# Reordering the first layer norm of a DiT block: x tile 3 ahead of tile 2, chunk 0's scale by itself, filler matmuls

## The chip, the cores and the metric

The kernel runs on one core of a Trainium2 chip. Its time is the time on the device for one execution, in microseconds (us); of several executions the median is given. Beside it stands the span, from the first to the last instruction of one profiled execution. Matmuls run on TensorE (PE in the profile; PEld is its weight load), elementwise work on VectorE (DVE), ScalarE (ACT) and GpSimd (POOL), and SyncE (SP) issues nearly all loads.

## The reference

One DiT block on x of 2 x 256 x 1152 (bf16), with a conditioning vector c per batch. Only the beginning matters here:

```python
mod = (_silu(c) @ w_mod).reshape(B, 6, 1, D)
shift_a, scale_a, gate_a, shift_m, scale_m, gate_m = [mod[:, i] for i in range(6)]
h = _layernorm(x, axis=-1) * (1 + scale_a) + shift_a
qkv = (h @ wqkv).reshape(B, N, 3, H, Dh)
...
x = x + gate_a * a
h2 = _layernorm(x, axis=-1) * (1 + scale_m) + shift_m
m = _gelu(h2 @ w_fc1) @ w_fc2
return x + gate_m * m
```

B is 2, N 256, D 1152, there are two heads of 576, and w_fc1 has 4608 columns. Between the lines shown stand softmax attention and the output projection wo.

## The kernel before

The 512 rows of x are four tiles of 128 rows (tiles 0 and 1 are batch 0, tiles 2 and 3 batch 1); the 1152 columns are nine chunks of 128. The kernel goes through the block in order: statistics and norm of x, k, shift, q, scores, softmax, v, attention, wo, second norm, fc1, fc2. It is written as straight-line code, and each engine executes its instructions in the order in which the source issues them (the loop at lines 777 to 787 fixes that by hand). So a wait at the head of an engine's queue holds all that stands behind it there.

What happens in the first 25 us:

- SP issues the four tiles of x (lines 85 and 86), then in turn pieces of w_scale_a (line 107: the columns for chunks 0 and 1, 2 and 3, 4 and 5, 6 and 7, and 8) and of w_k (line 104), all on one queue, with no wait between them.
- TensorE multiplies zeros in fp32 (`warm`, line 171), two times and later eight times more. Their result is not used.
- The statistics of tiles 0 and 2 are made on ScalarE: two passes with a running sum, of the difference to the row's first element and of its square (`act_stats`, line 202). VectorE and Pool make mean and variance of the sums (`act_mean`, `act_var`). Tiles 1 and 3 use bn_stats on VectorE, in three pieces of 384 columns (`stats_piece`).
- The inverse root for tiles 0 and 1 is a power on Pool (line 324), the one for tiles 2 and 3 is Ln and Exp on ScalarE (`ln_exp_rsqrt`).
- `norm1` writes the normalised tile xn on VectorE, the first 512 columns first (four chunks), the rest later. TensorE transposes it chunk by chunk into PSUM (`transpose_x`, line 258).
- `scale_group` makes the scale of some chunks: for each chunk nine matmuls of the weights w_scale_a with the vector silu(c), two columns wide (line 244). One is added on the way to SBUF, on ScalarE for chunks 0 and 1 (line 250), on VectorE for the others (line 251).
- `modulate` multiplies a transposed chunk of one batch (256 columns) by its scale while copying it from PSUM to hT0, on VectorE (line 264) or ScalarE (line 266). hT0 lies in the tile named big in the profile. The shift is left for later.
- `k_step(k, ...)` multiplies chunk k of hT0 with w_k for six accumulators pk of PSUM (line 274), for one batch or for both. PSUM has six accumulator buffers ("acc") and two for transposes and scales ("aux").

Chunks 0 to 3 are done batch by batch, in an order written out by hand at lines 332 to 362; from chunk 4 on a loop alternates scale group, transposes, modulation and k step, up to the evacuation of k.

Of the kernel before, what the change touches and what calls it, by code (L numbers as in the profile page):

```python
# [9 lines left out]
BF16 = mybir.dt.bfloat16  # L10
ACT = mybir.ActivationFunctionType
ALU = mybir.AluOpType
# [3 lines left out]
LN_EPS = 1e-5  # L16
# [3 lines left out]
def kernel(  # L20
# [11 lines left out]
    nc = tc.nc  # L32
    B, N, D = x.shape
# [3 lines left out]
    P = 128  # L37
    T = B * N
    NT = T // P
    TPB = N // P  # L40
    KD = D // P
# [11 lines left out]
    const = ctx.enter_context(tc.tile_pool(name="const", bufs=1))  # L53
# [6 lines left out]
    def acc_tile(shape, name, dt=FP32):  # L60
        return psum.tile(shape, dt, name=name, tag="acc", bufs=6)

    def aux_tile(shape, name, dt=FP32):
        return psum.tile(shape, dt, name=name, tag="aux", bufs=2)
# [17 lines left out]
    x_sb = act.tile([P, NT, D], BF16, name="x_sb", tag="x_sb")  # L82
    c_sb = act.tile([B * KD, P], BF16, name="c_sb")
    nc.scalar.dma_start(c_sb[:], c_v)
    for t in range(NT):
        nc.sync.dma_start(x_sb[:, t, :], x_v[:, t // TPB, t % TPB, :])  # L86

    zeros = const.tile([P, T], BF16, name="zeros")
# [10 lines left out]
    KM1 = 6  # L99
# [45 lines left out]
    hT0 = aT  # L145
# [11 lines left out]
    neg_half = const.tile([P, B], FP32, name="neg_half")  # L157
# [2 lines left out]
    nc.gpsimd.tensor_tensor(early[:], eps_t[:], neg_half[:, 0:1], op=ALU.pow)  # L160
    ones = const.tile([P, 1], FP32, name="ones")
    nc.gpsimd.memset(ones[:], 1.0)
    pc = aux_tile([P, B * KD], "pc", BF16)
    pwarm = acc_tile([P, T], "pwarm")

# [3 lines left out]
    def warm(n, dst):  # L169
        for _ in range(n):  # L170
            nc.tensor.matmul(dst[:, 0:T // 2], zeros32[:, 0:P], zeros32, start=True, stop=True)  # L171
# [13 lines left out]
    mv1 = small.tile([P, NT, 2], FP32, name="mv1", tag="mv1", bufs=1)  # L185
    rstd1 = small.tile([P, NT], FP32, name="rstd1", tag="rstd1", bufs=1)
# [3 lines left out]
    def stats_piece(t, j):  # L190
        nc.vector.bn_stats(stats1[t][:, j, :], x_sb[:, t, j * PW:(j + 1) * PW])
        if j == NPD - 1:
            nc.vector.bn_aggr(mv1[:, t, :], stats1[t][:].rearrange("p a b -> p (a b)"))


    dsum = small.tile([P, NT], FP32, name="dsum", tag="dsum", bufs=1)
    dsq = small.tile([P, NT], FP32, name="dsq", tag="dsq", bufs=1)
    dm2 = small.tile([P, NT], FP32, name="dm2", tag="dm2", bufs=1)

    def act_stats(t):  # L200
        for f, dst in ((ACT.Identity, dsum), (ACT.Square, dsq)):
            nc.scalar.activation(
                xns[t][:], x_sb[:, t, :], f, bias=x_sb[:, t, 0:1], scale=-1.0,
                accum_out=dst[:, t:t + 1],
            )

    def act_mean(t, eps):
        one = slice(t, t + 1)
        nc.vector.scalar_tensor_tensor(
            dm2[:, one], dsum[:, one], -1.0 / (D * D), dsum[:, one], op0=ALU.mult, op1=ALU.mult  # L210
        )
        if eps:
            nc.gpsimd.tensor_scalar_add(dm2[:, one], dm2[:, one], LN_EPS)
        nc.gpsimd.tensor_scalar(
            mv1[:, t, 0:1], dsum[:, one], -1.0 / D, x_sb[:, t, 0:1], op0=ALU.mult, op1=ALU.add
        )

    def act_var(t):
        one = slice(t, t + 1)
        nc.vector.scalar_tensor_tensor(  # L220
            mv1[:, t, 1:2], dsq[:, one], 1.0 / D, dm2[:, one], op0=ALU.mult, op1=ALU.add
        )

    def pair(t):
        return mv1[:, t:t + 2, 1:2].rearrange("p t o -> p (t o)"), rstd1[:, t:t + 2]

    def ln_exp_rsqrt(dst, var):
        nc.scalar.activation(dst, var, ACT.Ln, bias=eps_t[:], scale=1.0)
        nc.scalar.activation(dst, dst, ACT.Exp, scale=-0.5)

    def norm1(t, c0, c1):
        nc.vector.tensor_scalar(
            xns[t][:, c0:c1], x_sb[:, t, c0:c1], mv1[:, t, 0:1], rstd1[:, t:t + 1],
            op0=ALU.subtract, op1=ALU.mult,
        )


    scale_a = act.tile([P, KD, B], FP32, name="scale_a")

    def scale_group(k0, k1, tile_of=aux_tile):  # L240
        pm = tile_of([P, k1 - k0, B], "pm")
        for j in range(k0, k1):
            for k in range(KD):
                nc.tensor.matmul(  # L244
                    pm[:, j - k0, :], w_scale_a[:, k, j * P:(j + 1) * P], sT[:, k, 0:B],
                    start=(k == 0), stop=(k == KD - 1),
                )
        dst = scale_a[:, k0:k1, :]
        return lambda: (
            nc.scalar.activation(dst, pm[:], ACT.Identity, bias=ones[:]) if k0 == 0  # L250
            else nc.vector.tensor_scalar_add(dst, pm[:], 1.0)
        )

    def transpose_x(ks, ts):
        pt = aux_tile([P, len(ks), len(ts) * P], "pt", BF16)
        for j, t in enumerate(ts):
            for i, k in enumerate(ks):
                nc.tensor.transpose(pt[:, i, j * P:(j + 1) * P], xns[t][:, k * P:(k + 1) * P], ident[:])
        return pt

    def modulate(pt, i, k, b, j0, eng):
        dst, src, sc = hT0[:, k, b * N:(b + 1) * N], pt[:, i, j0:j0 + N], scale_a[:, k, b:b + 1]
        if eng == "d":
            nc.vector.tensor_scalar_mul(dst, src, sc)  # L264
        else:
            nc.scalar.mul(dst, src, sc)
# [3 lines left out]
    def k_step(k, c0=0, c1=T, m0=0, m1=KM1):  # L270
        for m in range(m0, m1):
            if k == 0 and c0 == 0:
                pk[m] = acc_tile([P, T], "pk")
            nc.tensor.matmul(  # L274
                pk[m][:, c0:c1], w_k[:, k, m * P:(m + 1) * P], hT0[:, k, c0:c1],
                start=(k == 0 and c0 == 0), stop=(k == KD - 1), skip_group_check=True,
            )
# [30 lines left out]
    CUT = 4 * P  # L308
    BT = [range(b * TPB, (b + 1) * TPB) for b in range(B)]

    def both(pt, k):
        for b, e in enumerate("da"):
            modulate(pt, 0, k, b, b * N, e)

    warm(8, pwarm)
    act_stats(0)
    act_stats(2)
    for j in range(NPD):
        stats_piece(1, j)
    act_mean(0, True)  # L320
    nc.gpsimd.tensor_scalar_add(mv1[:, 1, 1:2], mv1[:, 1, 1:2], LN_EPS)
    act_var(0)
    var, rstd = pair(0)
    nc.gpsimd.tensor_tensor(rstd, var, neg_half[:], op=ALU.pow)
    stats_piece(3, 0)
    norm1(0, 0, CUT)
    norm1(1, 0, CUT)
    stats_piece(3, 1)
    act_mean(2, False)
    stats_piece(3, 2)  # L330
    act_var(2)
    pt_a = transpose_x([0, 1], BT[0])
    add = scale_group(0, 2)
    add()
    modulate(pt_a, 0, 0, 0, 0, "d")
    var, rstd = pair(2)
    ln_exp_rsqrt(rstd, var)
    modulate(pt_a, 1, 1, 0, 0, "a")
    norm1(2, 0, CUT)
    norm1(3, 0, CUT)  # L340
    k_step(0, 0, N)
    k_step(1, 0, N, 0, 3)
    pt_c = transpose_x([0, 1], BT[1])
    modulate(pt_c, 0, 0, 1, 0, "d")
    modulate(pt_c, 1, 1, 1, 0, "a")
    norm1(0, CUT, D)
    norm1(1, CUT, D)
    k_step(1, 0, N, 3, KM1)
    k_step(0, N, T)
    add = scale_group(2, 4)  # L350
    pt_b = transpose_x([2, 3], BT[0])
    add()
    modulate(pt_b, 0, 2, 0, 0, "d")
    modulate(pt_b, 1, 3, 0, 0, "a")
    norm1(2, CUT, D)
# [6 lines left out]
    k_step(2, N, T)  # L362
    for k in range(3, KD):
        if k in (3, 5, 7):
            scale_group(k + 1, min(k + 3, KD))()
        if k < KD - 1:
            both(transpose_x([k + 1], range(NT)), k + 1)
        k_step(k)
# [143 lines left out]
    def attn_transpose(i):  # L512
        pair = attn_all[:, TPB * i:TPB * (i + 1), :].rearrange("p i n -> p (i n)")
        return nc.scalar.dma_start_transpose(attnT_all[:, i, :].rearrange("p (c n) -> p c n", n=P), pair)
# [242 lines left out]
    for gi, (n, t, c0, cw) in enumerate(groups):  # L757
# [3 lines left out]
        for kk in range(KF):  # L761
            j, r = divmod(n * KF + kk, 27)
# [3 lines left out]
                start=(kk == 0), stop=(kk == KF - 1),  # L766
# [11 lines left out]
    for ins in list(nc.cur_bb.bb.instructions)[first_traced:]:  # L778
        eng = ins.engine
# [38 lines left out]
```

## Time and profile before

| What | Value |
|---|---|
| Median of 4 runs | 244.13 us (243.87 to 245.23) |
| Profiled execution | 244.45 us |
| Its span | 242.7 us |
| Granted TensorE clock, mean | 1.000 |
| Bytes through the DMA queues | 53.29 MB, 220 GB/s on average |
| Landings of x tiles 0, 1, 2, 3 | 3.54, 4.28, 6.16, 7.10 us |
| Landings of w_scale_a, chunks 0-1 and 6-7 | 9.25 and 20.01 us |

All times of day in this document count from the span's start. The page of the profile gives first the busy time of each engine, then the same in 40 slices of the span, the DMA queues, the chain of work that ended last, and the costliest groups of instructions. The lines of an order of time are: start, length, engine, source line, operation, output<-input, shapes and number of instructions; in brackets the engine's idle time before it and what ended it. A busy TensorE is not TensorE at its peak. A matmul's length holds its latency too; where matmuls follow each other, what counts is the step from start to start.

### The profile page before, as it was taken

The page shows a single profiled execution, that of the slowest core. Times are in us where ns is not written, and L with a number is a line of the kernel's source. Part 1 is how long each engine was busy: PE and PEld are TensorE (multiplying, and loading weights), DVE is VectorE, ACT ScalarE, POOL GpSimd, SP SyncE. Part 2 cuts the span into 40 slices and gives each one's busy share as a digit, 9 for nine tenths or more (in the row PEclk, how much of TensorE's full clock was granted, in tenths as well). Part 3 has the DMA queues.
Part 4 walks back from the last instruction along what each step waited for, and adds up shares of the span by engine and source line. Part 5 has one row for each costly group of instructions (what it writes and reads, how often), then busy time and mean ns, then how long its engine had stood idle before and what let it go on. Part 6 is the DMA issues. An engine that isn't in the chain of part 4 may idle for free.

```text
span 242.7 us, 3988 instructions
## 1 busy us (share of the span) xinstructions
PE 237.0 (98%) x1698; PEld 145.5 (60%) x1698; DVE 91.1 (38%) x192; ACT 59.8 (25%) x120; POOL 27.8 (11%) x45
## 2 busy tenths in 40 slices
PE   8899999999999999999999999999999999999994
PEld 5775444466567666888854444444665665665674
DVE  4652442318416578831002999960010000000001
ACT  6632332307214032672422223332000000000000
POOL 2200000001400333200000000001121111111111
PEclk9999999999999999999999999999999999999999
DMA  6999999996499999239999999999200000000000
GB/s 204 316 319 319 379 365 392 389 393 215 99 307 397 389 375 153 41 65 340 392 389 393 343 327 297 261 327 296 97 16 16 20 16 16 19 18 16 26 25 16
DMA packets 48781, 53.29 MB, mean 220 GB/s; under 512 B 9587, under 2 KB 36475, under 8 KB 48763
## 3 DMA queue, kind: packets, MB, share of 16 engines
q1 hardware_dynamic: 41312, 50.14, 62.3%
q10 hardware_dynamic: 6939, 1.71, 5.1%
q0 software_dynamic: 512, 1.19, 1.8%
q8 instruction: 13, 0.21, 0.4%
q14 instruction: 5, 0.04, 0.1%
HBM read 50.14 MB, written 1.19 MB: 212 GB/s over the span
## 4 chain that ended last, share of the span: by engine, by line
PE 90%; SPq 4%; DMA 4%; issue 0%; DVE 0%; DVEq 0%
PE pacc L763 29%; PE pacc L707 29%; PE pacc L654 7%; PE pacc L563 7%; PE pq L485 7%; DMA w_scale_a<-in_w_mod_dram 4%; SPq L104 3%; PE pk L303 2%; PE pk L274 2%; PE pa L603 2%; PE ps_s L520 2%; PE pn L380 2%; SPq L86 1%; SPq L107 1%; PE pg L462 0%; PE pm L244 0%
## 5 line engine op out<-in xcount | busy, mean ns | idle before, releaser
L707 PE MATMUL pacc<-hT,w_f 128*128 128x256 bf16 (+1 forms) x432 | 70.5, 326 | 0.0
L763 PE MATMUL pacc<-w_f,gT 128*128 128x384 bf16 (+2 forms) x468 | 70.5, 314 | 0.0
L763 PEld LDWEIGHTS <-gT 128*128 128x128 bf16 x468 | 44.4, 98 | 26.2
L707 PEld LDWEIGHTS <-w_f 128*128 128x128 bf16 x432 | 42.2, 98 | 27.6
L769 DVE TENSOR_TENSOR tmp<-pacc,gate 128x384 f32<-128x384 f32 (+2 forms) x13 | 6.9, 527 | 65.6 <-PE pacc L763 57.3
L739 ACT ACTIVATE gT<-pacc 128x512 bf16<-128x512 f32 x24 | 14.3, 597 | 32.6 <-PE pacc L707 32.6
L433 DVE SCALAR_TENSOR_TENSOR part<-w_gate_m,s,part 128x1152 f32<-128x1152 bf16 x16 | 21.4, 1414 | 0.0
L654 PE MATMUL pacc<-w_o,big 128*128 128x384 bf16 x108 | 17.9, 326 | 0.0
L771 POOL TENSOR_TENSOR o_sb<-tmp,x 128x384 bf16<-128x384 f32 (+1 forms) x12 | 11.7, 971 | 54.0 <-DVE tmp L769 54.0
L485 PE MATMUL pq<-hT,w_q 128*128 128x512 bf16 x81 | 17.8, 379 | 0.0
L563 PE MATMUL pacc<-w_v,hT 128*128 128x384 bf16 x108 | 17.7, 326 | 0.0
L563 PEld LDWEIGHTS <-hT 128*128 128x128 bf16 x108 | 10.5, 98 | 7.1 <-issue 0.3
L654 PEld LDWEIGHTS <-big 128*128 128x128 bf16 x108 | 10.4, 98 | 7.2 <-issue 0.4
L274 PE MATMUL pk<-big,w_k 128*128 128x256 bf16 (+1 forms) x72 | 13.3, 326 | 0.9 <-DVE big L264 0.8
L485 PEld LDWEIGHTS <-w_q 128*128 128x128 bf16 x81 | 7.8, 98 | 9.4
L660 POOL TENSOR_TENSOR x<-tmp,x_sb 128x384 f32<-128x384 f32 x8 | 7.3, 913 | 27.1 <-DMA w_scale_m<-in_w_mod_dram 15.2
L431 DVE TENSOR_SCALAR part<-w_gate_m,s 128x1152 f32<-128x1152 bf16 x2 | 1.6, 819 | 21.9 <-DMA w_gate_m<-in_w_mod_dram 21.9
L274 PEld LDWEIGHTS <-w_k 128*128 128x128 bf16 x72 | 6.7, 98 | 4.5 <-issue 1.1
L171 PE MATMUL pwarm<-zeros 128*128 128x256 f32 x20 | 7.8, 564 | 1.2 <-DVE eps_t L93 1.2
L455 POOL DMA_DIRECT2D gates_dram<-nat_v x2 | 1.1, 534 | 67.6 <-DVE nat_v L453 67.6
L728 ACT ACTIVATE gT<-pacc 128x512 bf16<-128x512 f32 x12 | 6.5, 598 | 9.0 <-PE pacc L707 9.0
L476 POOL DMA_DIRECT2D gates_dram<-nat x4 | 2.3, 577 | 52.1 <-DVE nat L473 51.5
(94 smaller groups left out, 163.9 us busy)
## 6 DMA issues: line engine op xcount, KB each, us to landing
w_f<-in_w_fc_dram SPq DMA_DIRECT2D x12, 864.0 KB, 14.4
w_f<-in_w_fc_dram SPq DMA_DIRECT2D x3, 1728.0 KB, 7.9
w_f<-in_w_fc_dram SPq DMA_DIRECT2D x2, 2592.0 KB, 17.3
w_gate_a<-in_w_mod_dram SPq DMA_DIRECT2D x3, 864.0 KB, 11.7
w_v<-in_wqkv_dram SPq DMA_DIRECT2D x3, 864.0 KB, 13.9
w_o<-in_wo_dram SPq DMA_DIRECT2D x3, 864.0 KB, 14.0
w_shift_m<-in_w_mod_dram SPq DMA_DIRECT2D x3, 864.0 KB, 8.6
w_scale_m<-in_w_mod_dram SPq DMA_DIRECT2D x3, 864.0 KB, 13.3
```

Of the source, the lines that this page charges most:

```text
L104: nc.sync.dma_start(w_k[:, k0:k1, c0:c1], wqkv_v[:, k0:k1, D + c0:D + c1])
L171: nc.tensor.matmul(dst[:, 0:T // 2], zeros32[:, 0:P], zeros32, start=True, stop=True)
L274: nc.tensor.matmul(pk[m][:, c0:c1], w_k[:, k, m * P:(m + 1) * P], hT0[:, k, c0:c1], start=(k == 0 and c0 == 0), stop=(k == KD - 1), skip_g ...
L433: nc.vector.scalar_tensor_tensor(part[:, b, :], wg[:, k, :], s32[:, k, b:b + 1], part[:, b, :], op0=ALU.mult, op1=ALU.add,)
L485: nc.tensor.matmul(pq[m][:], w_q[:, k, m * P:(m + 1) * P], hT[:, k, :], start=(k == 0), stop=(k == KD - 1), skip_group_check=True,)
L563: nc.tensor.matmul(pacc[:], hT[:, k, t * P:(t + 1) * P], w_v[:, k, pnl * PW:(pnl + 1) * PW], start=(k == 0), stop=(k == KD - 1),)
L654: nc.tensor.matmul(pacc[:], aT[:, k, t * P:(t + 1) * P], w_o[:, k, c0:c1], start=(k == 0), stop=(k == KD - 1),)
L660: (nc.gpsimd if pool_add else nc.vector).tensor_tensor(x1[:, t, c0:c1], tmp[:], x_sb[:, t, c0:c1], op=ALU.add)
L707: nc.tensor.matmul(dst, w_f1[m // KD][:, k, ml * P:(ml + 1) * P], hT[:, k, c0:c1], start=start, stop=(k == KD - 1), **kw,)
L739: nc.scalar.activation(gT[:, m, :], pacc[:], ACT.Gelu_apprx_tanh)
L763: nc.tensor.matmul(pacc[:], gT[:, kk, t * P:(t + 1) * P], w_f2[j][:, r, c0 - n * PW:c0 - n * PW + cw], start=(kk == 0), stop=(kk == KF - 1),)
L771: (nc.vector if last else nc.gpsimd).tensor_tensor(o_sb[:], tmp[:], x1[:, t, c0:c0 + cw], op=ALU.add)
```

## The change

The change touches only what is issued in the first 13 us or so:

- x tile 3 is loaded ahead of tile 2.
- Tile 3's statistics are all issued ahead of the first norms; its inverse root is a power on Pool, by itself. Tile 2's stays with Ln and Exp on ScalarE, for one column instead of two.
- Tile 1 is normed ahead of tile 0, tile 3 ahead of tile 2.
- The scales of chunks 0 and 1 are two groups, with accumulators of the "acc" kind. Chunk 0's starts with a matmul of a row of ones, so that PSUM holds one plus the scale; VectorE multiplies the chunk of batch 0 by it straight from PSUM, and ScalarE copies it to SBUF later. Chunk 1's one is added on ScalarE as before, and its half of batch 0 is multiplied on VectorE instead of ScalarE.
- Two matmuls of zeros (128x512, bf16) are put into TensorE's order, one behind the scale matmuls and one behind tile 3's transposes.
- The transposes of chunks 0 and 1 for tile 3 stand ahead of the first k step, those for tile 2 between the first and the second; the second k step of batch 0 is no longer cut in two.

The core of the diff:

```diff
-    for t in range(NT):
+    for t in (0, 1, 3, 2):
         nc.sync.dma_start(x_sb[:, t, :], x_v[:, t // TPB, t % TPB, :])
...
+    ones_row = const.tile([1, P], BF16, name="ones_row")
+    nc.gpsimd.memset(ones_row[:], 1.0)
...
         for j in range(k0, k1):
+            if j == 0:
+                nc.tensor.matmul(pm[:, 0, :], ones_row[:], ones_row[:, 0:B], start=True, stop=False)
             for k in range(KD):
                 nc.tensor.matmul(
                     pm[:, j - k0, :], w_scale_a[:, k, j * P:(j + 1) * P], sT[:, k, 0:B],
-                    start=(k == 0), stop=(k == KD - 1),
+                    start=(k == 0 and j > 0), stop=(k == KD - 1),
                 )
...
+    def fill(n):
+        for _ in range(n):
+            nc.tensor.matmul(pwarm[:], zeros[:, 0:P], zeros[:], start=True, stop=True)
+
+    def pool_eps(t):
+        nc.gpsimd.tensor_scalar_add(mv1[:, t, 1:2], mv1[:, t, 1:2], LN_EPS)
+
+    def pool_rsqrt(t0, t1):
+        nc.gpsimd.tensor_tensor(
+            rstd1[:, t0:t1], mv1[:, t0:t1, 1:2].rearrange("p t o -> p (t o)"),
+            neg_half[:, 0:t1 - t0], op=ALU.pow,
+        )
...
-    act_mean(0, True)
-    nc.gpsimd.tensor_scalar_add(mv1[:, 1, 1:2], mv1[:, 1, 1:2], LN_EPS)
+    act_sq_mean(0)
+    nc.gpsimd.tensor_scalar_add(dm2[:, 0:1], dm2[:, 0:1], LN_EPS)
+    pool_eps(1)
+    stats_piece(3, 0)
     act_var(0)
-    var, rstd = pair(0)
-    nc.gpsimd.tensor_tensor(rstd, var, neg_half[:], op=ALU.pow)
-    stats_piece(3, 0)
+    pool_rsqrt(0, 2)
+    act_mean(0)
+    stats_piece(3, 1)
+    stats_piece(3, 2)
+    pool_eps(3)
+    pool_rsqrt(3, 4)
+    norm1(1, 0, CUT)
     norm1(0, 0, CUT)
-    norm1(1, 0, CUT)
-    stats_piece(3, 1)
-    act_mean(2, False)
-    stats_piece(3, 2)
+    pt_a = transpose_x([0, 1], BT[0])
+    act_sq_mean(2)
+    act_mean(2)
+    norm1(3, 0, CUT)
+    pm0, pm1 = [scale_group(k, k + 1, acc_tile) for k in range(2)]
     act_var(2)
-    pt_a = transpose_x([0, 1], BT[0])
-    add = scale_group(0, 2)
-    add()
-    modulate(pt_a, 0, 0, 0, 0, "d")
-    var, rstd = pair(2)
-    ln_exp_rsqrt(rstd, var)
-    modulate(pt_a, 1, 1, 0, 0, "a")
+    nc.vector.tensor_scalar_mul(hT0[:, 0, 0:N], pt_a[:, 0, :], pm0[:, 0, 0:1])
+    scale_add(pm1, 1, 2, "a")
+    modulate(pt_a, 1, 1, 0, 0, "d")
+    ln_exp_rsqrt(rstd1[:, 2:3], mv1[:, 2, 1:2])
+    nc.scalar.copy(scale_a[:, 0:1, :], pm0[:])
     norm1(2, 0, CUT)
-    norm1(3, 0, CUT)
+    fill(1)
+    pt_c = aux_tile([P, 2, N], "pt", BF16)
+    transpose_x([0, 1], [3], pt_c, 1)
+    fill(1)
     k_step(0, 0, N)
-    k_step(1, 0, N, 0, 3)
-    pt_c = transpose_x([0, 1], BT[1])
+    transpose_x([0, 1], [2], pt_c, 0)
+    k_step(1, 0, N)
     modulate(pt_c, 0, 0, 1, 0, "d")
     modulate(pt_c, 1, 1, 1, 0, "a")
     norm1(0, CUT, D)
     norm1(1, CUT, D)
-    k_step(1, 0, N, 3, KM1)
     k_step(0, N, T)
```

`act_mean` is split into `act_sq_mean` (VectorE) and `act_mean` (Pool), and the adding of the one is now `scale_add`; both do what they did.

More of the change, by code (lines that the diff above doesn't have):

```diff
@@ L205, in act_stats, with act_sq_mean @@
             )
-    def act_mean(t, eps):
+    def act_sq_mean(t):
         one = slice(t, t + 1)
@@ L211, in act_mean @@
         )
-        if eps:
-            nc.gpsimd.tensor_scalar_add(dm2[:, one], dm2[:, one], LN_EPS)
+    def act_mean(t):
         nc.gpsimd.tensor_scalar(
-            mv1[:, t, 0:1], dsum[:, one], -1.0 / D, x_sb[:, t, 0:1], op0=ALU.mult, op1=ALU.add
+            mv1[:, t, 0:1], dsum[:, t:t + 1], -1.0 / D, x_sb[:, t, 0:1], op0=ALU.mult, op1=ALU.add
         )
@@ L222, in act_var @@
         )
-    def pair(t):
-        return mv1[:, t:t + 2, 1:2].rearrange("p t o -> p (t o)"), rstd1[:, t:t + 2]
     def ln_exp_rsqrt(dst, var):
@@ L245, in scale_group, with scale_add, transpose_x @@
                     pm[:, j - k0, :], w_scale_a[:, k, j * P:(j + 1) * P], sT[:, k, 0:B],
-                    start=(k == 0), stop=(k == KD - 1),
+                    start=(k == 0 and j > 0), stop=(k == KD - 1),
                 )
[L248 to L256, printed above, removed]
+        return pm
+    def scale_add(pm, k0, k1, eng="d"):
+        if eng == "a":
+            nc.scalar.activation(scale_a[:, k0:k1, :], pm[:], ACT.Identity, bias=ones[:])
+        else:
+            nc.vector.tensor_scalar_add(scale_a[:, k0:k1, :], pm[:], 1.0)
+    def transpose_x(ks, ts, pt=None, j0=0):
+        if pt is None:
+            pt = aux_tile([P, len(ks), len(ts) * P], "pt", BF16)
+        for j, t in enumerate(ts, j0):
             for i, k in enumerate(ks):
@@ L347 @@
     norm1(1, CUT, D)
-    k_step(1, 0, N, 3, KM1)
     k_step(0, N, T)
-    add = scale_group(2, 4)
+    pm = scale_group(2, 4)
     pt_b = transpose_x([2, 3], BT[0])
-    add()
+    scale_add(pm, 2, 4)
     modulate(pt_b, 0, 2, 0, 0, "d")
@@ L364 @@
         if k in (3, 5, 7):
-            scale_group(k + 1, min(k + 3, KD))()
+            k1 = min(k + 3, KD)
+            scale_add(scale_group(k + 1, k1), k + 1, k1)
         if k < KD - 1:
```

## Prediction

> **What bounds the kernel now.** I read the page first, then the chain of waits, then the order of time of TensorE, VectorE and ScalarE over the first 21 us, and last the DMA queue around 18 us. From the page:
>
> ```profile
> span 242.7 us, 3988 instructions
> PE 237.0 (98%) x1698; PEld 145.5 (60%) x1698; DVE 91.1 (38%) x192; ACT 59.8 (25%) x120; POOL 27.8 (11%) x45
> ```
>
> TensorE is idle for only 5.7 us: 1.2 before its first matmul, about 3 after its last one, and 1.3 in between. The matmul idle in between lies wholly before 21 us, in the stretch that the change edits. So no edit of it can win more than that, and what it wins must survive to the first point where TensorE waits for something else. Two lines of TensorE's order of time show the two places (start, length, engine, line, operation; in brackets the idle time before and what ended it):
>
> ```profile
> 9.29 0.60 PE L244 MATMUL pm<-sT,w_scale_a 128*128 128x2 bf16 x18
> 10.70 1.14 PE L274 MATMUL pk<-big,w_k 128*128 128x256 bf16 x9 [0.80 <-DVE big L264]
> ...
> 18.21 1.46 PE L274 MATMUL pk<-big,w_k 128*128 128x512 bf16 x6
> 20.05 0.60 PE L244 MATMUL pm<-sT,w_scale_a 128*128 128x2 bf16 x18 [0.38 <-DMA w_scale_a<-in_w_mod_dram]
> ```
>
> The first idle, 0.80, is what the change works on. The second is a DMA: the scale columns for chunks 6 and 7 land at 20.01. The chain of waits (start, length, what) agrees, and it does not go through 10.70 at all:
>
> ```profile
> 11.20 8.81 DMA w_scale_a<-in_w_mod_dram
> 20.01 0.05 issue
> 20.05 0.60 PE pm L244 x18
> 20.66 0.25 PE pt L258 x4
> 20.90 1.29 PE pk L274 x6
> ```
>
> Behind 20.05 the chain is TensorE's own work down to 239.5 us. The last matmul ahead of 20.05 starts at 19.293 and the next could start 0.216 later (the step between 512-column matmuls there), at 19.51. So TensorE arrives 0.54 early in this execution: **slack 0.54**.
>
> **The change, part by part.** Where a step has the same semaphore latency as now, I keep the offset that the trace shows (0.02 to 0.09).
>
> *x tile 3 ahead of tile 2.* SP issues the same four loads (0.38 to 0.43 each) ahead of the same weights, so the weight queue does not move. The landings are 3.54, 4.28, 6.16 and 7.10; tiles 3 and 2 swap the last two. Tile 3's three bn_stats on VectorE start at 6.18 instead of 7.12, and step by 0.47. Tile 2's two ScalarE passes start at 7.12 instead of 6.20; two passes with their reads took from 6.20 to 8.91, 2.71, so the square sum is there at 9.83.
>
> *Statistics ahead of the norms.* VectorE: bn_stats at 6.18, tile 0's variance at 6.65 (its square sum is there at 6.30), two bn_stats to 7.77, the aggregate to 8.04 (0.24; the next one can follow 0.15 after its start). Pool's root for tiles 0 and 1 (0.72) starts at about 6.9 as now and ends at 7.61, the mean at 7.87 (0.26), and both are hidden by the bn_stats. The norms of tiles 1 and 0 (0.41 each, stepping by 0.33) run from 7.96 to 8.69 instead of 7.68 to 8.41. TensorE's transposes need both: 0.28 later for VectorE. It costs nothing, because the warming matmuls hold TensorE until 8.876 in any case (8.69 plus 0.05 to the weight load plus 0.1 is 8.84). This cover is thin: 0.03.
>
> *Root of tile 3 on Pool.* The addition of eps costs 0.20 and the root lies between 0.58 (the 128x1 root of line 160) and 0.72 (the 128x2 one). From 8.04: ready at 8.95 to 9.1. Tile 3's norm runs to about 9.5 instead of 11.51. Pool has nothing else to do; tile 2's mean behind it takes 0.26, and is wanted only at 10.7.
>
> *Chunk 0's scale alone.* Now the 18 scale matmuls end at 9.90, ScalarE adds one, and only then VectorE multiplies:
>
> ```profile
> 10.00 0.26 ACT L250 ACTIVATE scale_a<-pm,ones 128x4 f32<-128x4 f32 x1 [1.08 <-PE pm L244]
> ...
> 10.30 0.35 DVE L264 TENSOR_SCALAR big<-pt,scale_a 128x256 bf16<-128x256 bf16 x1 [0.60 <-ACT scale_a L250]
> ```
>
> With the one added by a matmul with a row of ones (one more 25 ns step beside 18; its weight load 0.1 lies in the 0.20 wait for the weights), nine matmuls end at 9.7 and VectorE reads the scale from PSUM. But tile 2's variance stands ahead in VectorE's queue and waits for the square sum at 9.83. So it runs at 9.86 and the multiplication at 9.95 to 10.30. Its price with a scalar from PSUM no row shows: between 0.35 (the same shape here) and 0.51 (with the 0.16 of the small PSUM read of line 251 on top); I take 0.35, the same operation and shape. The first k matmul can start at 10.35 instead of 10.70.
>
> *Fillers.* Two matmuls of 512 columns, 0.216 each at the step seen from 16.7 on (0.427 if the clock were at its early half). After the scale matmuls (last start 9.73): filler, two transposes of tile 3 (0.055 each), filler: done at 10.4. They lie in the wait for VectorE and cost 0.05 of it at most, 0.5 in the slow case.
>
> *Order of the k steps.* The first matmuls now run at 10.40 to 11.05. VectorE multiplies chunk 1 (0.35, at 10.3, the scale from ScalarE at 10.26), and norms tile 2 when its root is there: Ln follows ScalarE's scale at 10.16, Exp ends at 10.68, norm 10.73 to 11.15. Transposes at 11.2, chunk 1's six matmuls 11.3 to 12.0. VectorE's first half-tile of batch 1 is done at 11.9, just ahead of TensorE. ScalarE's late copy of chunk 0's scale (0.16 to 0.26, about 10.9) releases the sixth accumulator, wanted at 10.95: 0 to 0.05. The second six end at 12.6, and the next scale group, which started at 13.159, starts at about **12.62: 0.54 earlier**. That takes in the 0.115 idle at 12.5, which goes too. Its weights are there: 12.28 by the landing marks. The groups behind keep their distance: chunks 4 and 5 at about 15.5 (weights at 15.39), and arrival at the wait for chunks 6 and 7 at 18.97 instead of 19.51.
>
> **The sum.** 0.54 won by 12.6, and all of it handed to the DMA at 20.01: TensorE then waits about 1.08 for the same landing. Sum for the profiled execution (244.45, span 242.7): 0. That execution stands 0.32 above the median of 244.13, so the forecast is **244.1**, with 243.8 to 244.5 for this case.
>
> Why the landing should stay: the sixteen landing marks of that transfer stand at 17.17 to 18.44 for fifteen, and at 20.01 for the last. In between the queue holds one instruction fetch:
>
> ```profile
> q1 hardware_dynamic: 1150, 0.61, 112.8%
> q8 instruction: 1, 0.02, 3.6%
> ```
>
> (window 17 to 19: packets, MB, share). It starts at 17.66 and takes 1.15 of one DMA engine. The change puts six instructions more on TensorE ahead of it (three matmuls with loads) and TensorE runs 0.54 earlier, so I expect the fetch about 1 us earlier. It still stands ahead of the last packets of this transfer on its engine, and delays them as much. The Trainium skill, "Runtime: NRT & Kernel Launch", section "Instruction fetch mechanics", says that crossing a 16 KiB block of instructions costs a DMA tail-bump that is mostly hidden. The trace speaks against it here, with the last mark 1.57 behind the fifteenth; by the rule the landing would be near 18.5 and the sum -1.08 instead of 0.
>
> **Rivals.**
> 1. *The DMA is not the end* (faster). If in the timed runs the scale columns land before 18.97, the slack of 0.54 and the gain of 0.54 both count. Without any DMA wait the old kernel would take 244.45 - 0.54 = 243.91, and the fastest of its runs is 243.87, so some runs seem to go that way. Landing in between gives part of it. Bound: 1.08, since chunk 8's columns land at 22.28 and would then be wanted at 22.26. Time 243.0 to 243.8; chance 0.22.
> 2. *The clock drops in the longer wait* (slower). The wait at 20.0 grows from 0.54 to 1.08. Against it: the 0.80 idle at 9.9 left the granted clock at 1.00. For it: early matmuls step by 0.427, and by 0.216 only from 7.4, 6.2 after the first one, so a drop would cost half of 3 to 6 us: 1.6 to 3.1, from the point at which the idle is long enough to lose it. Time 245.7 to 247.2; chance 0.06. The Trainium skill ("TensorE: Matmul & The Clock Gate", section "What's actually happening") wants an idle window of about 3.4 us for that, three times this wait.
> 3. *The new chain is late* (slower, or no better). Tile 2's variance blocks VectorE's queue ahead of the first k matmul, and everything behind it, if ScalarE's passes are late. It decides only from 1.08 late on, that is from a square sum after 10.9, so with the upper prices above (0.16, 0.5) added up the time still doesn't move; a late clock in some runs would add to it. Time 244.5 to 245.5; chance 0.09.
>
> **How the numbers follow.** The forecast has 0.63. Rival 1 pulls the low end to 243.1, rival 3 the high end to 245.0; left out are rival 2, half of rival 3 and the tail of rival 1, about 0.15. About 0.5% (1.22 us) can be told from no change by a measurement of this kernel: under 242.9 lies only what goes past rival 1's bound, where the clock's early half lasts longer in the old kernel than in this execution: 0.08, taken out of rival 1. Over 245.35: rival 2 and a third of rival 3, 0.09. The rest is 0.83.
>
> **What will show it.** Right: the first k matmul near 10.4 with little idle before it, the second scale group near 12.6, arrival near 19.0, an idle of about 1 us ended by the DMA of the scale columns, their landing still at 20.0, then the same times to the end. Wrong: a landing that moves with the instruction fetch; matmuls stepping by 0.427 behind 20; an idle at 10 us that stays, ended by VectorE waiting on ScalarE. The forecast fails most easily at the landing.

## The result, and the profile after

| | before | after |
|---|---|---|
| Median of all executions | 244.32 us (78 executions) | 243.86 us (54) |
| Ratio (that of the means, 244.55 and 243.88) | | 0.9973, 95% interval 0.9964 to 0.9981 |
| Profiled execution, its span | 244.45, 242.7 us | 243.41, 241.6 us |
| Executions over 245.0 us | 23 of 78 | 1 of 54 |
| Median of the others | 244.19 us | 243.85 us |

The change makes the kernel 0.27% faster on average. The last two rows matter as much as the first: the executions of the old kernel fall into two groups with a gap between 244.86 and 245.10, and the change acts on each of them differently. For the 78 only the times are on record. For the changed kernel, for the runs below and for the 105 executions of the old kernel beside them the granted clock of each execution is there too, and it makes the same division: 0.992 or 0.993 on average over the execution in the upper group, 0.998 to 1.000 in the lower one. In the runs below I divide by that clock.

Span and chain of the changed kernel (in the chain: start, length, what):

```profile
span 241.6 us, 3999 instructions
PE 237.1 (98%) x1701; PEld 145.3 (60%) x1701; DVE 91.4 (38%) x193; ACT 59.7 (25%) x120; POOL 28.9 (12%) x48
```

```profile
2.57 6.61 DMA w_scale_a<-in_w_mod_dram
9.17 0.05 issue
9.22 0.60 PE pm L245 x18
...
19.20 0.43 PE pm L245 x18
```

The chain no longer touches the columns of chunks 6 and 7. It leaves the DMA at 9.17, with the landing of the first scale columns, and from there to 238.5 us it is TensorE alone, but for 0.04 at 10.39. TensorE's order of time, at the places that the prediction showed for the old kernel:

```profile
9.22 0.60 PE L245 MATMUL pm<-sT,w_scale_a 128*128 128x2 bf16 x18
9.68 0.38 PE L321 MATMUL pwarm<-zeros 128*128 128x512 bf16 x1
...
10.43 0.81 PE L278 MATMUL pk<-big,w_k 128*128 128x256 bf16 x6
...
12.69 0.59 PE L245 MATMUL pm<-sT,w_scale_a 128*128 128x2 bf16 x18
...
17.74 1.46 PE L278 MATMUL pk<-big,w_k 128*128 128x512 bf16 x6
19.04 0.59 PE L245 MATMUL pm<-sT,w_scale_a 128*128 128x2 bf16 x18
```

No line carries an idle bracket any more. The second scale group starts at 12.69 (13.16 before), the one for chunks 6 and 7 at 19.04 (20.05 before). Of the 1.01, 0.07 is an earlier start at 9.22, 0.40 the shorter way from the first to the second scale group (3.47 instead of 3.87), and 0.54 the DMA wait, which is gone: the columns landed at 18.39, not at 20.01.

### The profile page after: what moved, and what is told of

Same layout as the page of the kernel before. It is cut to its first block, busy times and chain, and to the rows that moved or that the text cites. A ratio compares the mean times of both kernels' runs of the same rounds, so it can differ in the third digit from the quotient of the medians.

```text
span 241.6 us, 3999 instructions
## 1 busy us (share of the span) xinstructions
PE 237.1 (98%) x1701; PEld 145.3 (60%) x1701; DVE 91.4 (38%) x193; ACT 59.7 (25%) x120; POOL 28.9 (12%) x48
## 3 DMA queue, kind: packets, MB, share of 16 engines
q0 software_dynamic: 512, 1.19, 1.8%
HBM read 50.14 MB, written 1.19 MB: 212 GB/s over the span
## 4 chain that ended last, share of the span: by engine, by line
PE 95%; DMA 3%; SPq 1%; DVE 0%; issue 0%; DVEq 0%
PE pacc L732 29%; PE pacc L788 29%; PE pacc L679 7%; PE pacc L588 7%; PE pq L510 7%; PE pk L278 5%; DMA w_scale_a<-in_w_mod_dram 3%; PE pk L307 2%; PE pa L628 2%; PE ps_s L545 2%; PE pn L405 2%; PE pm L245 1%; PE pt L262 1%; SPq L86 1%; PE pg L487 0%; PE pwarm L321 0%
```

## The experiments

Each kernel's executions ran beside the old kernel's on the same chip, e1 to e4 on one chip, e5 to e8 on another, e9 to e12 on a third; a comparison with "the changed kernel's" median joins the first comparison and e5, and so goes across chips. The old kernel's lower group stood at 243.99 to 244.05 on these three, at 244.19 in the first comparison. Medians are those of the lower group unless said otherwise; "fell" counts the executions with a mean clock of 0.992 or 0.993. Intervals of differences are 95%, by resampling. The filler matmuls added below have results that are not used.

### What the fillers do

**e1: the changed kernel without fillers.**

```diff
-    fill(1)
...
-    fill(1)
```

> The changed kernel without its two filler matmuls; all else as there. Theory (clock): the old kernel's executions fall into two groups, 55 of 78 at 243.6 to 244.9 (median 244.19) and 23 of 78 at 245.1 to 245.8; the changed one has 53 of 54 in the lower group (median 243.85). The upper group are executions in which TensorE loses its full clock for one window of some 3.4 us behind the quiet stretch from 9 to 10.7 us, 1.7 us of time less the 0.54 of slack. The fillers keep that stretch busy. Without them the upper group should come back in part (the quiet stretch is still 0.35 us shorter than in the old kernel), 5 to 30 in 100, with a mean clock near 0.993 in those executions, and the lower group should stay at 243.85 with the first k matmul near 10.4. Rival (landing): the upper group are executions in which the scale columns for chunks 6 and 7 land late, and the fillers do nothing: no upper group, mean clock 1.00 whatever the time.

4 of 12 fell, all at 245.6 to 245.8; with the fillers 2 of 66 fell (the first comparison and e5), so in this kernel the fillers hold the clock. The lower group stands at 243.86. The trace happens to be of an execution that fell (245.62). TensorE in four stretches of it (stretch, its length, TensorE's busy time and instructions, granted clock, DMA share, GB/s):

```profile
5.70:9.10 3.40, 2.93 (x17) 1.00 1.02 309
9.10:12.50 3.40, 2.11 (x33) 1.00 1.15 321
12.60:15.90 3.30, 3.30 (x36) 0.50 1.15 318
16.00:19.40 3.40, 3.40 (x47) 1.00 1.18 306
```

The clock's own records say: full from 5.74 to 12.57, half to 15.98, full again. So the windows are 3.41 us long, and the quiet one is 9.15 to 12.57. What is quiet in it shows in the order of time:

```profile
9.97 0.60 PE L245 MATMUL pm<-sT,w_scale_a 128*128 128x2 bf16 x18 [0.81 <-DMA w_scale_a<-in_w_mod_dram]
10.44 0.27 PE L262 MATMUL pt<-ident,xn 128*128 128x128 bf16 x2
11.19 0.82 PE L278 MATMUL pk<-big,w_k 128*128 128x256 bf16 x6 [0.48 <-DVE big L356]
...
12.12 2.33 PE L278 MATMUL pk<-big,w_k 128*128 128x256 bf16 x12
```

Two waits and 18 matmuls of two columns; the last line's twelve matmuls take 2.33 where the same twelve take 1.49 at full clock. If I count as streaming the matmuls of more than two columns, less 0.16 of latency each where nothing follows, this window streams for 1.33 us, or 39%. In the thirteen other traces of this study the first two windows from the clock's release on stream for 1.60 or more, and none of them fell. So by this count the line lies between 39% and 47%; that rests on a single window that fell, and TensorE's busy share separates it as well (62% here, 70% or more in the others), so which of the two counts is open. A window at half clock costs up to 1.7 us of work. In this trace the way from the first scale matmul to chunk 8's scale group is 14.75 long, where the changed kernel's is 13.30, so 1.45 was lost; the groups of the old kernel stand 1.20 apart.

The Trainium skill ("TensorE: Matmul & The Clock Gate", section "HAM oscillation — how this bites in real kernels") gives as its rule that idle gaps over some 3.4 us are to be avoided. The window's length agrees (3.41), the rule is too mild: here the longest single idle time in the window that fell was 0.81. A longer one did not do it: in e9's trace below TensorE sat idle for 1.90, from 8.29 to 10.19, but two windows, counted from the clock's release at 5.91, meet at 9.33, each holds only a part of it, and the clock stayed.

**e2: two fillers alone in the old kernel.**

```diff
     add = scale_group(0, 2)
+    for _ in range(2):
+        nc.tensor.matmul(pwarm[:], zeros[:, 0:P], zeros[:], start=True, stop=True)
     add()
```

> The old kernel with two filler matmuls of 512 columns behind its 18 scale matmuls, in the 0.80 us idle; nothing else changed. Theory (clock): the upper group of executions (23 of 78 of the old kernel above 245.0) disappears, under 5 in 100, and the lower group keeps its median of 244.19; the first k matmul stays at 10.70. Rival (landing): the share above 245.0 stays near 30 in 100. Rival (cost): the fillers delay something and the lower group rises by up to 0.4.

3 of 12 fell, against 8 of 35 beside it; lower group 243.93 against 243.99. The expectation missed: two fillers in the old kernel did not take the falls away. Nor did they cost anything that shows. The explanation is argued, since the trace of this run did not fall: where the clock wakes early (4.7 to 5.9 us in five of the fourteen traces), the warming matmuls end early too, and TensorE waits twice in one window: for the first scale columns, then for VectorE. The fillers stand only in the second wait. In this run's trace the first wait ended at 9.34, where one window ends as well, so that the two waits lay in two windows.

**e8: four fillers in the old kernel, one of them ahead of the scale matmuls.**

```diff
+    nc.tensor.matmul(pwarm[:], zeros[:, 0:P], zeros[:], start=True, stop=True)
     add = scale_group(0, 2)
+    for _ in range(3):
+        nc.tensor.matmul(pwarm[:], zeros[:, 0:P], zeros[:], start=True, stop=True)
     add()
```

> The old kernel with one filler ahead of its first 18 scale matmuls and three behind them. Theory (clock, mended): the clock falls when TensorE streams for less than about half of a 3.41 us window (1.33 in the one window that fell, 1.82 or more in those that did not), and windows that begin between 8.0 and 9.1 take in both the wait for the first scale columns and the one for VectorE. Two fillers behind left too little (3 of 12 still fell), four should do: at most 1 in 12 with a mean clock of 0.993, where the old kernel has about 3 in 10. The lower group stays within 0.1 of the old kernel's or rises by up to 0.1. Rival: the fall has another cause, and 3 or more of 12 stay.

0 of 12 fell, against 8 of 35 beside it; lower group 244.16 against 243.99 beside it (difference 0.17, -0.09 to 0.33).

```profile
9.75 0.81 PE L336 MATMUL pwarm<-zeros 128*128 128x512 bf16 x3
10.69 1.14 PE L274 MATMUL pk<-big,w_k 128*128 128x256 bf16 x9
...
20.07 0.60 PE L244 MATMUL pm<-sT,w_scale_a 128*128 128x2 bf16 x18 [0.40 <-DMA w_scale_a<-in_w_mod_dram]
```

The fillers run to 10.56, and the first k matmul starts at 10.69, as early as in the old kernel's first trace. With 12 executions, 0 against an expected 2 to 3 is an indication and no proof that enough streaming holds the clock in the old kernel too; it brought nothing else that shows. In the kernels with two fillers below the clock fell in 1 of 36 (e5, e6, e7) and 0 of 12 (e4), but also in 2 of 12 (e10) and 5 of 12 (e9): fillers alone do not settle it.

### What the reordering does

**e5: the changed kernel again**, unchanged.

> The changed kernel once more, as the measure for the two runs beside it. What the traces so far say: from the first scale matmul (released by the landing of the scale columns of chunks 0 and 1) to the second scale group it takes 3.47 us, where the old kernel takes 3.87, so the lower group should stand 0.3 to 0.4 below the old kernel's; executions above 245.0 at most 1 in 12, with a mean clock of 0.993.

Lower group 243.81 (beside it 243.99), 1 of 12 fell; first to second scale group 3.40. The gain stands on this chip too: 0.18 (0.03 to 0.53) against the old kernel beside it. With this run the changed kernel's lower group has 64 executions with a median of 243.84. Against all 145 of the old kernel it is 0.20 lower (0.13 to 0.38), in the first comparison alone 0.34 (0.23 to 0.52).

**e7: the scales of chunks 0 and 1 together again.**

```diff
-    pm0, pm1 = [scale_group(k, k + 1, acc_tile) for k in range(2)]
+    pm01 = scale_group(0, 2)
...
-    nc.vector.tensor_scalar_mul(hT0[:, 0, 0:N], pt_a[:, 0, :], pm0[:, 0, 0:1])
-    scale_add(pm1, 1, 2, "a")
+    scale_add(pm01, 0, 2, "a")
+    modulate(pt_a, 0, 0, 0, 0, "d")
```

(The row of ones goes too, and so does the late copy of chunk 0's scale.)

> The changed kernel with one part undone: the scales of chunks 0 and 1 are one group again, ScalarE adds the one to both, and VectorE multiplies chunk 0 only then. The fillers stay. Theory: from the first scale matmul to the first k matmul it takes 1.4 us again instead of 1.21, and to the second scale group about 3.66 instead of 3.47; the lower group rises by 0.2 against the run beside it, with no more than 1 in 12 above 245.0. Rival (prediction's): tile 2's variance holds VectorE's queue either way, and the time stays within 0.1.

```profile
9.78 0.60 PE L243 MATMUL pm<-sT,w_scale_a 128*128 128x2 bf16 x18 [0.66 <-DMA w_scale_a<-in_w_mod_dram]
...
11.19 0.81 PE L276 MATMUL pk<-big,w_k 128*128 128x256 bf16 x6
...
13.26 0.59 PE L243 MATMUL pm<-sT,w_scale_a 128*128 128x2 bf16 x18
```

The first k matmul comes 1.41 behind the first scale matmul, as expected, but the second scale group 3.48 behind it, where the changed kernel has 3.40 to 3.47. The expected 0.2 is not there: what is won at the first k matmul is lost in the wait for tile 2's transposes, which hang on Exp and tile 2's norm either way. The times do not settle it: lower group 244.09, 0.25 above the changed kernel's, with an interval from -0.05 to 0.52. The traced execution started at 9.78, late, and lost another 0.25 between 78 and 98 us, a stretch that the edit does not touch. None of 12 fell.

**e10: tile 3's root back on ScalarE.**

```diff
-    pool_eps(3)
-    pool_rsqrt(3, 4)
...
-    norm1(3, 0, CUT)
...
-    ln_exp_rsqrt(rstd1[:, 2:3], mv1[:, 2, 1:2])
+    ln_exp_rsqrt(rstd1[:, 2:4], mv1[:, 2:4, 1:2].rearrange("p t o -> p (t o)"))
...
     norm1(2, 0, CUT)
-    fill(1)
+    norm1(3, 0, CUT)
+    fill(2)
...
-    transpose_x([0, 1], [3], pt_c, 1)
-    fill(1)
     k_step(0, 0, N)
     transpose_x([0, 1], [2], pt_c, 0)
+    transpose_x([0, 1], [3], pt_c, 1)
     k_step(1, 0, N)
```

> The changed kernel with tile 3's root back on ScalarE (Ln and Exp for tiles 2 and 3 together), its norm behind tile 2's, and its two transposes behind the first k step; the scale of chunk 0 by itself and both fillers stay (both in one place). Theory (norm): what shortens the way from the first to the second scale group, 3.87 to 3.47 us, is that tile 3's norm (0.33) and two transposes (0.11) no longer stand between Exp and the second k step. Then this kernel takes about 3.85 again, although its first k matmul still comes 1.2 behind the first scale matmul, and the lower group rises to 244.1 to 244.2. Rival (scale): chunk 0's scale alone makes the gain, and the kernel stays at 3.5 to 3.6.

```profile
9.51 0.60 PE L245 MATMUL pm<-sT,w_scale_a 128*128 128x2 bf16 x18
...
10.52 0.82 PE L278 MATMUL pk<-big,w_k 128*128 128x256 bf16 x6
11.46 0.61 PE L262 MATMUL pt<-ident,xn 128*128 128x128 bf16 x4
...
13.23 0.59 PE L245 MATMUL pm<-sT,w_scale_a 128*128 128x2 bf16 x18
```

The first k matmul is as early as in the changed kernel (1.01 behind the first scale matmul), and yet the way to the second scale group is 3.72 long, because all four transposes now stand at 11.46 behind both norms. The lower group is 244.18, 0.34 above the changed kernel's (0.25 to 0.56), and level with the old kernel beside it (244.05). So tile 3's norm, with its root and its two transposes (this run undoes the three together), is the part that carries the gain: 0.25 of the 0.40. What makes the remaining 0.15 is not shown; chunk 0's scale alone was worth next to nothing in e7's trace (0.01 to 0.08). 2 of 12 fell.

The traces side by side, without e1's, bear that out. The way runs from the first scale matmul to chunk 8's scale group:

| Kernel, traces | The way | From there to the span's end |
|---|---|---|
| old, with the wait at 20 (first trace, e8) | 14.26, 14.28 | 219.12 |
| old, without it (e2, e3, e11, e12) | 13.70 to 13.71 | 219.06 to 219.13 |
| changed (first trace, e5, e4, e6, e9) | 13.23 to 13.33 | 219.05 to 219.12, in e6 219.25 |
| e7 | 13.32 | 219.37 |
| e10 | 13.56 | 219.11 |

What lies behind chunk 8's group is the same in all but two traces. So but for these two a traced execution's length is set by when its first scale matmul starts and by this way.

**e9: x loaded in the old order.**

```diff
-    for t in (0, 1, 3, 2):
+    for t in range(NT):
```

> The changed kernel with x loaded in the old order 0, 1, 2, 3 and nothing else undone. Tile 3 then lands last, at 7.1 to 7.5 instead of 5.6 to 6.1, and its bn_stats stand ahead of tile 0's variance and of the norms on VectorE: the norms end at about 9.6 instead of 8.7, the scale matmuls start at about 9.95 instead of 9.2 to 9.4, the second scale group at about 13.3 instead of 12.7. Expected: lower group 0.3 to 0.6 above the changed kernel's 243.85, so the same as the old kernel or slower. Rival: the first scale columns (9.2 to 9.9) hide it, and it costs under 0.1.

```profile
10.19 0.38 PE L262 MATMUL pt<-ident,xn 128*128 128x128 bf16 x4 [1.90 <-DVE dm L211]
10.51 0.17 PE L243 MATMUL pm<-ones_row 1*128 1x2 bf16 x1
10.61 0.60 PE L245 MATMUL pm<-sT,w_scale_a 128*128 128x2 bf16 x18
```

Tile 3 landed at 7.62, its statistics hold the norms, and the first transposes wait 1.90 us, longer than the scale columns (9.56). The scale matmuls start at 10.61, where 9.95 was expected. The lower group is 244.62, 0.78 above the changed kernel's (0.52 to 1.05), more than the 0.3 to 0.6 expected, and above the old kernel's, and 5 of 12 fell in spite of the fillers. The load order is a condition of the rest.

### The wait at 20 us

**e3: the columns of chunks 6 and 7 ahead of w_k of chunk 5, old kernel.**

```diff
+        if k0 == 6:
+            load_k(5, 6, 0, KM1 * P)
-        for a, z in [(0, 1), (1, 2)] if k0 == 0 else [(k0, k1)]:
+        for a, z in {0: [(0, 1), (1, 2)], 4: [(4, 5)]}.get(k0, [(k0, k1)]):
             load_k(a, z, 0, KM1 * P)
```

> The old kernel with one edit of the loads: w_k for chunks 4 and 5 is split, and the scale columns for chunks 6 and 7 are issued between the two halves, so ahead of w_k of chunk 5. Theory: the wait at 20.0 us goes, and each execution that waited there gains up to 0.54: lower group from 244.19 to about 243.9, with the columns landing near 18 to 19.4 and the upper group kept (about 30 in 100). w_k of chunk 5 then lands at 18.4 to 20.0 and is wanted at about 20.2. Rival: the landing was not binding in most executions, and the lower group stays within 0.1 of 244.19.

Lower group 244.06 against 243.99 beside it; 4 of 12 fell. The columns landed at 18.12 and there was no wait, but the executions gained nothing that shows (difference 0.08, -0.24 to 0.56). So it is likely that in most executions of the old kernel that wait was not there; with it the gain was to be up to 0.54.

**e12: the old kernel again**, unchanged.

> The old kernel unchanged, for a second trace. If the fetch always stands at 17.7 in it, the columns land at 20.0 again and TensorE waits 0.4 to 0.5 for them; if the wait in the first trace was that execution's, the landing is near 18.4 and there is no wait.

```profile
9.78 0.60 PE L244 MATMUL pm<-sT,w_scale_a 128*128 128x2 bf16 x18 [0.42 <-DMA w_scale_a<-in_w_mod_dram]
11.19 1.14 PE L274 MATMUL pk<-big,w_k 128*128 128x256 bf16 x9 [0.80 <-DVE big L264]
...
20.00 0.59 PE L244 MATMUL pm<-sT,w_scale_a 128*128 128x2 bf16 x18
```

The 0.80 is there again, the wait at 20 is not. The group starts at 20.00 here only because the chain started 0.49 later, at 9.78. The columns landed at 18.93, and the instruction fetch stood at 16.67 instead of 17.66, in the same program. 1 of 8 fell.

**e11: twelve matmuls of two columns in the old kernel's idle time.**

```diff
     add = scale_group(0, 2)
+    for _ in range(12):
+        nc.tensor.matmul(pwarm[:, 0:2], zeros[:, 0:P], zeros[:, 0:2], start=True, stop=True)
     add()
```

> The old kernel with twelve matmuls of two columns (24 instructions, about 0.3 us) in TensorE's 0.80 us idle behind the first scale matmuls; they stream next to nothing, so the clock's falls should stay at about 3 in 10. TensorE's instruction fetch of 17.66 should come 1 to 2 us earlier. In the traces so far the scale columns of chunks 6 and 7 landed at 20.0 where the fetch stood at 17.7 (2 of 2) and at 18.1 to 19.1 where it stood at 16.1 to 17.3. Expected by that: landing near 18.4, no wait at 20, a profile some 0.5 shorter than the old kernel's where the rest is equal. Rival (prediction's): an earlier fetch delays the columns as much, and they land near 20.0 again.

The fetch stood at 16.49, the columns landed at 18.43, no wait. But since e12 shows an equally early fetch without the added matmuls, this run does not say what moves the fetch. Over the eleven traces with one order of these two transfers (columns, then w_k): where the fetch stood at 17.66 or 17.71 (the old kernel's first trace, e8) the columns landed at 20.0; where it stood at 16.1 to 17.3 (nine traces) they landed at 18.1 to 19.1. That the fetch is the cause is not shown, but an earlier fetch did not come with the late landing in any of the nine, against the prediction's view that it costs the same. The lower group is 244.07 (244.05 beside it) and 3 of 12 fell (6 of 35 beside it): twelve matmuls of two columns did not take the falls away. Since two of 512 columns did not either (e2), this does not tell small ones from large.

**e4 and e6: the same edit of the loads in the changed kernel, twice.**

> The changed kernel with the same edit of the loads (scale columns of chunks 6 and 7 ahead of w_k of chunk 5). Theory: the executions between 243.6 and 244.3 of the changed kernel are those that wait for the columns; they gather at 243.3 to 243.5, and the median falls from 243.85 to about 243.5. w_k of chunk 5 is wanted at about 19.7 and lands at 18.4 to 20.0, so up to 0.3 may stay. Rival: the spread comes from the clock's wake-up, not from the landing, and the median stays within 0.1 of 243.85.

> The changed kernel with the scale columns of chunks 6 and 7 issued ahead of w_k of chunk 5, once more, now beside the changed kernel on one chip. If a late landing of those columns (20.0 us in the profile of the old kernel, 18.4 in three others) costs the changed kernel time in some executions, the highest of the lower group go (none above 244.0) and the median falls by 0.1 to 0.3 against the run beside it. If the spread comes from the start (the first scale columns landed between 9.2 and 9.9 us in the traces), the two are the same within 0.1.

243.61 and 243.50, none of 24 fell, none above 243.99; against the old kernel beside them 0.9974 (0.9957 to 0.9991) and 0.9969 (0.9954 to 0.9983). Against the 64 executions of the changed kernel the 24 are 0.29 lower (0.11 to 0.50); on one chip, e6 against e5, it is 0.31, with an interval from -0.08 to 0.51. So it is the fastest of the versions tried, and the only one here that beats both kernels. Why it does is only argued, for its own way in the traces (13.33, 13.24) is no shorter: the changed kernel arrives at this point 0.4 earlier than the old one and so waits in more executions, but neither of its two traces shows the wait.

## Why the prediction was right and where it failed

It forecast no change that 0.5% can tell, 244.1 within 243.1 to 245.0. The time is 243.86, and the move of -0.27% is real. That the time lies within the range is in part luck: the step that kept the sum at 0 failed, and what came in its place was small enough for the range. By its steps:

- **What bounds the kernel, where an edit can win:** right. All of the change's gain in the traced execution lies before 20 us; from 19.04 on the chain is TensorE's own, as it was from 20.05 on, and 222.6 us of span follow in both. But its bound, the 1.3 us of idle time, left out what a fall of the clock costs.
- **The parts' prices:** right to some hundredths. Tile 3's root 0.58 on Pool; the multiplication from PSUM 0.35, as taken; the late copy 0.14 (forecast 0.16 to 0.26); the first k matmul at 10.43 (forecast 10.40), held by tile 2's variance in VectorE's queue, which waited 0.61 for ScalarE:

```profile
9.95 0.16 DVE L222 SCALAR_TENSOR_TENSOR mv<-dsq,dm 128x1 f32<-128x1 f32 x1 [0.61 <-ACT xn L204]
10.03 0.35 DVE L356 TENSOR_SCALAR big<-pt,pm 128x256 bf16<-128x256 bf16 x1
...
10.77 0.41 DVE L231 TENSOR_SCALAR xn<-x_sb,mv,rstd 128x512 bf16<-128x512 bf16 x1
```

- **0.54 by the second scale group:** the size was off. The group came 0.47 earlier (12.69), 0.07 of it from an earlier start; the way from the first scale matmul was to take 3.33 (12.62 less 9.29) and took 3.47. In this trace the group hangs on tile 2, whose square sum was there at 9.92 instead of 9.83.
- **The cause of the 0.54:** half wrong. The prediction put the first k matmul in front; e7 and e10 show that what counts in the traces is tile 3's norm and transposes out of Exp's wake, that is, no longer waiting for Exp on ScalarE.
- **"All of it handed to the DMA at 20.01":** this step failed. The wait belonged to the one execution that had been profiled; e12 has none, and 1 other of the 11 traces has it (e8). The argument that the landing stays wherever the fetch stands was false: the fetch came 0.41 earlier (17.25; forecast about 1 us), and the columns landed at 18.39. What may be left of the wait is small: e4 and e6 are 0.29 below the changed kernel.
- **Rival 1** (the DMA is not the end) happened, in the profiled execution nearly to its bound (1.04 against 1.08 between the two profiled times). In the median it gave less than the 243.0 to 243.8 put down for it, likely because the old kernel seldom waited (e3).
- **Rival 2** (the clock) had the mechanism and the wrong place. The prediction looked for a fall behind the longer wait at 20 us and took the clock of 1.00 behind the 0.80 idle as evidence of safety. It read one execution: 23 of 78 of the old kernel's stand in the upper group, 1.2 us higher, and the change leaves 1 of 54 there. One of the four times that the prediction had, 245.23, was of that group. The idle window of about 3.4 us that it cited was not needed: 0.81 was the longest idle time in e1's window.

The two effects add up in the first comparison: 0.34 on the lower group, and 23/78 less 1/54, times 1.2, or 0.33. Together 0.67, which is the ratio's 0.27% of 244.3 (0.66). On the second chip (e5) the lower group's share was 0.18.

What stays open: what chunk 0's scale alone is worth in the times (0.25, -0.05 to 0.52), what makes the last 0.15 of the way, what sets the instruction fetch's time, and how often the columns land late in executions without a trace.

## What to carry to other kernels

Before a wait of one profiled execution is taken as a floor, a second trace of the same kernel should show it; a DMA landing that differs by 1.6 us between executions is not a bound. Look at the spread of the times for groups, and at the granted clock of each execution: a part of the executions may pay for a quiet stretch that the profiled one got away with. And to shorten a chain, find the norm or transfer that hangs on its last link, not the first instruction that starts late: here moving one norm and its transposes out of Exp's wake was worth what an earlier first matmul was not.

## What the runs showed of the hardware that was not expected

- The clock falls to half for one window of 3.41 us after a window in which TensorE streamed for 39% of the time, though its longest idle time was 0.81 (e1, one window); at 47% it did not fall, with an idle time of 1.90 that lay across two windows (e9).
- An instruction fetch of 16 KB, 1.15 to 1.19 us long, came at 17.66 and at 16.67 in one program. Where it stood at 17.66 or 17.71, the last of the sixteen landing marks of the scale columns came 1.6 us behind the fifteenth; in the nine traces with it at 16.11 to 17.25, 0.07 to 0.45 behind.
- The start moves between executions: the fourth tile of x landed at 6.96 to 7.93, the first scale columns at 9.02 to 9.93. The chain hangs on them: in the old kernel's four traces without the wait at 20 the span less the landing of the first scale columns is 232.8 to 232.9. The lower group's spread is about 1 us, so most of it may come from there.
